# Weight preparation spread 4, 5 and 4 a tick, with the first weight loads held back, in a fused scan and two-MLP kernel

## The chip, the cores and the metric

The kernel runs on one core of a Trainium2 chip. A core has a matrix engine (TensorE, PE in the profile; the loading of its stationary operand is shown as PEld), a vector engine (VectorE, DVE), a scalar engine (ScalarE, ACT), a general engine (GpSimd, POOL) and a synchronisation engine (SyncE, SP). Each engine works through its own queue of instructions in order. DMA transfers are issued from the queues of SP, ACT and POOL. The metric is the device time of one execution in microseconds (us).

## The reference

Three computations follow one another. First a scan over a sequence of 768 positions for 4 batches and 8 heads, with a decay per position, in chunks:

```python
cum = np.cumsum(la, axis=-1)                       # la = log(clip(a))
L = np.exp(cum[:, :, :, None] - cum[:, :, None, :]) * causal
M = np.einsum('bhin,bhjn->bhij', Cc, Bc) * L
y_intra = np.einsum('bhij,bhjd->bhid', M, xc)
y_inter = np.einsum('bhin,bhnd->bhid', Cc, state) * decay_to_i[..., None]
...
state = decay_full[:, :, None, None] * state + np.sum(Bx, axis=2)
```

Its output, 3072 tokens of 256 numbers, goes through two layers in float32:

```python
h = x @ w_in                                       # 256 -> 2048
x = (np.maximum(h, 0.0) + alpha * np.minimum(h, 0.0)) @ w_out
gate = 1.0 / (1.0 + np.exp(-(x @ w_gate)))         # 256 -> 1536
out = (gate * (x @ w_val)) @ w_out2
```

## The kernel before, in words

The scan is cut into chunks of 96 positions (`T`), 8 per batch and 32 in all (`NCH`). The loop over `i` in 33 ticks works on them in a staggered way: in tick `i` VectorE makes the weighted scores `mt(i)` (`ev_weigh`, L324) and the state's factor `bd(i)` (L331), TensorE makes the decay `d(i+1)` (L298), which ScalarE turns into `lt(i+1)` by an exponential (L303), TensorE makes the output `yd(i-1)` (L346, L352), which ScalarE copies out as the next state (L359) and as the layer's input `x1` (L360), and TensorE makes the scores `cb(i+1)` (L317). The logarithms' running sum, called cum here, is made at the start for all chunks in two parts (`parts`). Its first three chunks go by small DMAs straight to `dl` and `dr` (`load_cum`, L261 and L262), the later ones through DRAM (`cum_d`). A small constant `pick` that the two parts need comes by a DMA from the tile `picks` (L548).

From tick `lead` = 7 on (`go` is true then; `at` counts the steps), the same ticks also hold steps of the first layer, one step per tick: `step_in` makes `h` for 512 tokens and 128 hidden columns (six matmuls, L391), then ScalarE and VectorE make `t` (L396), `g` (L398) and its two halves `gh` and `gl` (L407, L408), and `step_out` adds the step before into `acc` (six matmuls, L430). The first 16 steps use columns 0 to 1023 for token blocks 0 and 1 (`half` is 8 steps), the next 16 steps the other columns. After the 33 ticks the rest of the first layer and the second layer run without the scan.

The weights come in 64-bit floats and are made into two float32r parts on the chip. They are handled in groups (one 128x2x256 tile each, 512 KB of DMA): `queue` holds `win0, wout0, win1, wout1, ...`, 16 groups for the first layer (`first2`) and 18 for the second. `take_up` issues a group's load on the POOL queue (L118) into the ring `raw` of `RAWS` = 3 buffers. `work()` hands out one instruction, or nothing, of the conversion at a time, `OPS` = 7 to a group: handout 0 scales on ScalarE (`mag<-raw`, L130, the present group and the next one), 1 shifts (L155, or two at L158), 2 copies the high part on ScalarE (L145), 3 clips (L163), 4 makes the low part (L147), 5 and 6 put sign and bits together (L165, L170); 2 and 4 finish the group before. `feed(n, ...)` hands out n of them; `need(g)` hands out at once whatever group g still lacks. A `raw` buffer is free again after its handout 6, and `take_up` may be `RAWS` groups ahead.

What sets the order around the change is this written-out loop, nothing else: before tick 7 each tick hands out `EARLY` = 6 (3 after `ev_decay`, 3 at the tick's end), from tick 7 on 1 and 2.

Of the kernel before, what the change touches and what calls it, by code (L numbers as in the profile page):

```python
# [8 lines left out]
F32 = mybir.dt.float32  # L9
# [9 lines left out]
T = 96  # L19
# [8 lines left out]

WG = 256

RAWS = 3

OPS = 7

EARLY = 6

NX = 6
NC = 4
# [6 lines left out]
def kernel(  # L45
# [21 lines left out]
    nc = tc.nc  # L67
    NB, H, S = a.shape
    NT, DM = out.shape
# [13 lines left out]
    NR = NB * H  # L83


    KD = T + 2 + 2 * H

    bf = lambda t: t.bitcast(F32)
# [11 lines left out]
    x1 = cpool.tile([128, KT, NT], F32, name="x1")  # L100
# [12 lines left out]

    def take_up(most=RAWS):

        while taken[0] < min(len(queue), worked[0] // OPS + most):
            raw = ring.tile([128, 2, WG, 2], U32, tag="raw", name="raw", bufs=RAWS)
            nc.gpsimd.dma_start(  # L118
                out=raw.rearrange("p k f w -> p k (f w)"), in_=words(queue[taken[0]][1])
            )  # L120
            raws[taken[0]] = raw
            taken[0] += 1
# [11 lines left out]
    def work():  # L134


        g, op = divmod(worked[0], OPS)
        if g < len(queue):
            flips = queue[g][2]
            low, high = (raws[g][:, :, :, w] for w in range(2))  # L140
        if op in (2, 4):
            if g > 0:
                dst, m = queue[g - 1][0], mags[g - 1]
                if op == 2:
                    nc.scalar.copy(dst[:, 0], m)  # L145
                else:
                    nc.vector.tensor_tensor(dst[:, 1], m, bf(dst[:, 0]), op=ALU.subtract)  # L147
        elif g == len(queue):
            pass
        elif op == 0:  # L150
            scale(g)
            scale(g + 1)
        elif op == 1:
            if flips is None:
                nc.vector.tensor_scalar(low, low, 29, None, op0=ALU.logical_shift_right)  # L155
            else:
                for i in range(2):
                    nc.vector.tensor_scalar(  # L158
                        low[:, i], low[:, i], 29, flips[:, i:i + 1],
                        op0=ALU.logical_shift_right, op1=ALU.bitwise_xor,  # L160
                    )
        elif op == 3:
            nc.vector.tensor_scalar(mags[g], mags[g], TOP, -TOP, op0=ALU.min, op1=ALU.max)  # L163
        elif op == 5:
            nc.vector.scalar_tensor_tensor(  # L165
                low, high, 0x80000000, low, op0=ALU.bitwise_and, op1=ALU.bitwise_xor
            )
        else:
            m = mags[g].bitcast(U32)
            nc.vector.scalar_tensor_tensor(  # L170
                m, m, 3, low, op0=ALU.logical_shift_left, op1=ALU.bitwise_or
            )
        worked[0] += 1
        take_up()
# [4 lines left out]
    def feed(n, groups):  # L179

        for _ in range(n):
            if worked[0] < ready(groups - 1):
                work()
# [8 lines left out]
    first2 = len(queue)  # L192
# [7 lines left out]
    apool = actx.enter_context(tc.tile_pool(name="apool", bufs=1))  # L200
# [10 lines left out]
    left_c = misc[0:KD, T:T + W]  # L211
    eye_d = k_misc[0:N, c0 + T:c0 + T + N]
    pick = apool.tile([2 * NR, 1], F32, name="pick")
    picks = apool.tile([1, NR, 2], F32, name="picks")
    ones_t = apool.tile([2 * NR, T], F32, name="ones_t")

    parts = apool.tile([2 * NR, S], F32R, name="parts")

    a_t, cum = (x1[0:2 * NR, i, NT - S:NT] for i in range(2))
    xs = [apool.tile([W, H * (D + N)], F32, name=f"xs{i}") for i in range(NX)]  # L220
    dl = [apool.tile([KD, W], F32R, name=f"dl{i}") for i in range(NC)]
    dr = [apool.tile([KD, H, T], F32R, name=f"dr{i}") for i in range(NC)]
# [7 lines left out]
    def load_x(c):  # L230

        b, k = divmod(c, CPB)
        t = xs[c % NX]
        nc.sync.dma_start(out=t[0:T], in_=xb[b, k * T:(k + 1) * T, :])
        if k == 0:
            nc.gpsimd.memset(t[T:W, 0:H * D], 0.0)

    def load_bc(c):


        if c < ND:
            BC[c] = aring.tile([128, W + 4 * T], F32, tag="bc0", name="bct", bufs=3)
            nc.sync.dma_start(out=BC[c], in_=bc0[:, c])
        elif (c - ND) % G == 0:
            g = (c - ND) // G
            nc.sync.dma_start(
                out=bt[g % NG][:, :, 0:T], in_=bc[g][:, 0].rearrange("p (g t) -> p g t", t=T)
            )
            src = bc[g][:, 1].rearrange("(m q) t -> q m t", q=NP)
            dst = ct[g % NG].rearrange("(m q) b t -> q m b t", q=NP)  # L250
            for q in range(NP):
                nc.sync.dma_start(out=dst[q][:, q], in_=src[q])
# [34 lines left out]
    def store_cum():  # L287
        nc.sync.dma_start(
            out=cum_d.rearrange("b h l s -> (b h l) s"), in_=bf(parts)
        )  # L290
# [3 lines left out]
    def ev_decay(c):  # L294

        d = psum.tile([W, 2, 512], F32, tag="d", name="d")
        for e in range(2):
            nc.tensor.matmul(  # L298
                d[:, e, 0:4 * T], dl[c % NC], dr[c % NC][:, 4 * e:4 * e + 4, :],
                start=True, stop=True,  # L300
            )
        LT[c] = t = aring.tile([W, H, T], F32, tag="lt", name="lt", bufs=2)
        nc.scalar.activation(  # L303
            t.rearrange("j (e h) t -> j e (h t)", e=2), d[:, :, 0:4 * T], AF.Exp
        )
# [97 lines left out]
    def halves(key):  # L403
        g = gt[key]
        gh = ring.tile([128, BL], F32R, tag="gh", name="gh", bufs=3)
        gl = ring.tile([128, BL], F32R, tag="gl", name="gl", bufs=3)
        nc.scalar.copy(gh, g)  # L407
        nc.vector.tensor_tensor(gl, g, bf(gh), op=ALU.subtract)  # L408
        gt[key] = gh, gl
# [3 lines left out]
    half = NF1 // 2  # L413
# [53 lines left out]
    def moe2_out(k, f):  # L467
# [8 lines left out]
        if last:  # L476

            prods.sort(key=lambda v: v[1] // 2)
            sb = ring.tile([128, 2, 2, DM], F32, tag="raw", name="osb", bufs=RAWS)
        for n, (i, tt) in enumerate(prods):  # L480
# [24 lines left out]
    with tc.manual_schedule():  # L505
# [28 lines left out]
        def load_a(e, s):  # L534
            for l in range(2):
                e.dma_start(
                    out=a_t[l:2 * NR:2, s], in_=a.rearrange("b h s -> (b h) s")[:, s]
                )

        def load_eye(i):  # L540
            nc.gpsimd.dma_start(
                out=xs[i][T:W, H * D:].rearrange("s (h n) -> s h n", n=N),
                in_=eye_d.unsqueeze(1).broadcast_to([N, H, N]),
            )

        load_a(nc.sync, pieces[0])
        load_a(nc.scalar, slice(T, S))
        nc.gpsimd.dma_start(out=pick, in_=picks)  # L548
        nc.scalar.activation(warm[:, 0:1], ones_t[:, 0:1], AF.Ln)
        nc.sync.dma_start(out=misc, in_=k_misc[:, c0:])  # L550
        load_bc(0)
        load_x(0)
        load_eye(0)
        nc.gpsimd.dma_start(out=alpha_sb, in_=alpha)
        load_eye(1)
        take_up(1)
        nc.gpsimd.dma_start(out=units_c, in_=k_misc[:, 0:N])

        def setup_dl(i):
            nc.scalar.copy(dl[i], left_c)  # L560
# [36 lines left out]
        load_bc(1)  # L597
        load_cum(1)
        load_x(1)
        ev_decay(0)  # L600
        take_up(2)
        setup_dl(2)
# [6 lines left out]
        load_x(2)  # L609
        store_cum()  # L610
        load_eye(2)
        take_up()
        setup_dl(3)
        setup_mask(3, nc.scalar)
# [10 lines left out]
        at = 0  # L625
        for i in range(NCH + 1):
            go = i >= lead
            if i < NCH:
                ev_weigh(i)
            if i == 0:  # L630
                for j in range(NG):
                    nc.scalar.activation(
                        bt[j][:, :, T:W], units_c.unsqueeze(1).broadcast_to([128, G, N]),
                        AF.Copy, scale=2.0,
                    )
            if i + 3 < NCH:
                load_x(i + 3)
                load_bc(i + 3)
            if i + 4 < NCH:
                load_cum(i + 4)  # L640
            if at > 0:
                halves(steps[at - 1])
            if i + 1 < NCH:
                ev_decay(i + 1)
            feed(1 if go else EARLY // 2, first2)
            if go:
                step_in(at, "h")
            if i > 0:
                ev_out(i - 1)
            if i + 1 < NCH:  # L650
                ev_scores(i + 1)
            if go:
                if at > 0:
                    step_out(at - 1, two=False)
                splits(at)
                at += 1
            feed(2 if go else EARLY // 2, first2)

            if i == lead // 2:
                split_x("m1", 0, 0, BL // 2)  # L660
            if i == lead - 1:
                split_x("m1", 0, BL // 2, BL)

            if i == -(-2 * BL // T):
                split_x("m1", 1)
# [101 lines left out]
```

## Time and profile before

| | us |
|---|---|
| median of 3 runs | 669.73 |
| lowest and highest | 668.87 and 670.18 |
| profiled execution | 671.24 |
| its span | 669.5 |

| engine | busy us | share of the span |
|---|---|---|
| PE | 636.6 | 95% |
| DVE | 389.7 | 58% |
| ACT | 333.5 | 50% |
| POOL | 33.7 | 5% |

The profile shows one execution. The engines' busy times overlap, so they don't add up to the span; what an engine's idle time costs depends on the place where it lies. The granted clock is the share of TensorE's full speed: 1.00 is 2.4 GHz and 0.50 is 1.2 GHz.

### The profile page before, as it was taken

How to read it: one execution, taken by the hardware profiler on the slowest of the kernel's cores; microseconds unless marked ns; L12 is line 12 of the kernel's file. 1: busy time of each engine (PE TensorE's matmuls, PEld its weight loads, DVE VectorE, ACT ScalarE, POOL GpSimd, SP SyncE). 2: the span in 40 equal slices, each digit the busy share in tenths (PEclk: the TensorE clock that was granted, in tenths of full speed). 3: DMA queues.
4: the chain of work that ended last, by engine and by line, in shares of the span. 5: the costliest groups of instructions: out<-in, count | busy, mean ns of one | idle time of the engine just before them, and what ended most of it. 6: DMA issues, size and time to landing. Idle time of an engine off the chain costs nothing.

```text
span 669.5 us, 9604 instructions
## 1 busy us (share of the span) xinstructions
PE 636.6 (95%) x3744; PEld 503.6 (75%) x3744; DVE 389.7 (58%) x636; ACT 333.5 (50%) x628; POOL 33.7 (5%) x53
## 2 busy tenths in 40 slices
PE   1779999998999999999999999999999999999997
PEld 0336667675788888888888888888888888888885
DVE  5677768687688887888677433443433433433433
ACT  4667777766556666656556333332332333332322
POOL 6110100000000000000000000000000000000000
PEclk9769999999999999999999999999999999999999
DMA  5653333412112221121000000000000000000000
GB/s 171 205 149 111 89 114 93 124 54 64 31 34 63 64 63 37 58 64 64 0 1 0 1 1 0 32 0 1 33 0 1 32 0 1 32 0 1 32 1 31
DMA packets 19751, 31.03 MB, mean 46 GB/s; under 512 B 7418, under 2 KB 15226, under 8 KB 19706
## 3 DMA queue, kind: packets, MB, share of 16 engines
q0 software_dynamic: 5184, 17.89, 8.7%
q1 hardware_dynamic: 14394, 12.36, 6.4%
q8 instruction: 29, 0.48, 0.3%
q10 hardware_dynamic: 128, 0.18, 0.1%
q14 instruction: 16, 0.13, 0.1%
HBM read 27.04 MB, written 3.34 MB: 45 GB/s over the span
## 4 chain that ended last, share of the span: by engine, by line
PE 89%; DVE 3%; issue 2%; ACT 2%; DMA 2%; POOL 0%; ACTq 0%; SPq 0%; POOLq 0%; DVEq 0%
PE acc L430 20%; PE h L391 19%; PE gate L457 15%; PE val L457 15%; PE po L485 10%; PE po L490 5%; PE cb L317 3%; PE yd L352 1%; PE d L298 1%; DMA raw<-in_moe_w_out_dram 1%; PE yd L346 1%; DMA raw<-in_moe_w_in_dram 1%; DVE mt L324 1%; ACT xs L359 0%; DMA pick<-picks 0%
## 5 line engine op out<-in xcount | busy, mean ns | idle before, releaser
L391 PE MATMUL h<-xh,win 128*128 128x512 f32 x576 | 148.2, 393 | 3.1 <-ACT xh L382 1.7
L464 DVE TENSOR_TENSOR p<-val,s 128x512 f32<-128x512 f32 x72 | 49.8, 692 | 138.5 <-PE val L457 136.7
L391 PEld LDWEIGHTS h<-xh,win 128*128 128x128 f32 x576 | 109.0, 190 | 25.1 <-ACT xh L382 2.1
L430 PE MATMUL acc<-gh,wout 128*128 128x512 f32 x384 | 106.7, 400 | 1.8 <-DVE wout L147 1.8
L398 DVE SCALAR_TENSOR_TENSOR g<-h,salpha,t 128x512 f32<-128x512 f32 x96 | 72.0, 750 | 51.2 <-ACT t L396 50.8
L457 PE MATMUL gate<-xh,w2gate 128*128 128x512 f32 x360 | 92.8, 393 | 0.0
L430 PEld LDWEIGHTS acc<-gh,wout 128*128 128x128 f32 x384 | 70.6, 189 | 28.4 <-ACT t L396 10.0
L457 PE MATMUL val<-xh,w2val 128*128 128x512 f32 x360 | 91.4, 389 | 0.0
L407 ACT CAST gh<-p 128x512 fp32r<-128x512 f32 x72 | 44.6, 620 | 93.7 <-DVE p L464 93.7
L396 ACT ACTIVATE t<-h,sign 128x512 f32<-128x512 f32 x96 | 66.0, 688 | 50.5 <-PE h L391 50.0
L462 ACT ACTIVATE s<-gate 128x512 f32<-128x512 f32 x72 | 43.0, 597 | 92.8 <-PE gate L457 92.8
L407 ACT CAST gh<-g 128x512 fp32r<-128x512 f32 x96 | 59.6, 621 | 44.8 <-DVE g L398 44.8
L457 PEld LDWEIGHTS val<-xh,w2val 128*128 128x128 f32 x360 | 67.6, 188 | 14.3
L408 DVE TENSOR_TENSOR gl<-g,gh 128x512 fp32r<-128x512 f32 x96 | 66.1, 689 | 15.0 <-ACT gh L407 13.9
L408 DVE TENSOR_TENSOR gl<-p,gh 128x512 fp32r<-128x512 f32 x72 | 49.8, 691 | 41.2 <-ACT gh L407 41.1
L457 PEld LDWEIGHTS gate<-xh,w2gate 128*128 128x128 f32 x360 | 64.0, 189 | 10.6
L485 PE MATMUL po<-w2out,gh 128*128 128x512 f32 x240 | 64.2, 389 | 0.0
L430 PE MATMUL acc<-gl,wout 128*128 128x512 f32 x192 | 59.8, 393 | 0.0
L485 PEld LDWEIGHTS po<-w2out,gh 128*128 128x128 f32 x240 | 45.1, 188 | 9.3
L430 PEld LDWEIGHTS acc<-gl,wout 128*128 128x128 f32 x192 | 36.3, 189 | 7.8
L490 PEld LDWEIGHTS po<-w2out,gl 128*128 128x128 f32 x240 | 36.7, 189 | 4.7
L490 PE MATMUL po<-w2out,gl 128*128 128x256 f32 x240 | 38.1, 282 | 0.0
(83 smaller groups left out, 570.0 us busy)
## 6 DMA issues: line engine op xcount, KB each, us to landing
raw<-in_moe_w_out_dram POOLq DMA_DIRECT2D x14, 512.0 KB, 4.4
xs<-in_xb_dram SPq DMA_DIRECT2D x32, 144.0 KB
raw<-in_moe_w_in_dram POOLq DMA_DIRECT2D x8, 512.0 KB, 4.4
raw<-in_moe_w_gate_dram POOLq DMA_DIRECT2D x6, 512.0 KB, 4.1
raw<-in_moe_w_val_dram POOLq DMA_DIRECT2D x6, 512.0 KB, 4.1
out_dram<-osb SPq DMA_DIRECT2D x12, 256.0 KB
bt<-in_bc_dram SPq DMA_DIRECT2D x7, 192.0 KB
ct<-in_bc_dram SPq DMA_DIRECT2D x28, 48.0 KB
```

The costliest lines, as they stand in the source:

```text
L317: nc.tensor.matmul(cb[:, e, 0:4 * T], left, right, start=True, stop=True)
L391: nc.tensor.matmul(h, w[:, wl, kt, :], xh["m1", k][:, xl, kt, :], start=(i == 0 and kt == 0), stop=(i == 2 and kt == KT - 1),)
L396: nc.scalar.activation(t, h, AF.Identity, scale=sign[:, f:f + 1])
L398: nc.vector.scalar_tensor_tensor(g, h, salpha[:, f:f + 1], t, op0=ALU.mult, op1=ALU.max)
L407: nc.scalar.copy(gh, g)
L408: nc.vector.tensor_tensor(gl, g, bf(gh), op=ALU.subtract)
L430: nc.tensor.matmul(acc[k][:, m], w[:, wl, m * 128:(m + 1) * 128], g, start=(first and i == 0), stop=(last and i == 2),)
L457: nc.tensor.matmul(p, w[:, wl, kt, :], xh["m2", k][:, xl, kt, :], start=(i == 0 and kt == 0), stop=(i == 2 and kt == KT - 1),)
L462: nc.scalar.activation(s, gate, AF.Sigmoid)
L464: nc.vector.tensor_tensor(p, val, s, op=ALU.mult)
L485: nc.tensor.matmul(o[e][:, u].rearrange("p (l d) -> p l d", l=2), ph[:, ts], w, start=(f == 0), stop=False, skip_group_check=True,)
L490: nc.tensor.matmul(o[e][:, u, 0:DM], pl[:, ts], w[:, 0, :], start=False, stop=last, skip_group_check=True,)
```

## The change

There are four buffers for weights instead of three. Ticks before `lead` hand out 4 weight instructions (2 and 2) instead of 6, the first eight ticks with a step 5 (2 and 3) and the later ones 4 (2 and 2) instead of 3 (1 and 2). `picks` moves into an unused stretch of `x1`, and its DMA to the ScalarE queue. The first weight load is issued ahead of the small constants on POOL; the second and third stand behind two new copies on POOL that read the cum rows of chunk 1 and of chunk 2 (`seen`), so that they are issued when those rows have landed.

```diff
-RAWS = 3
+RAWS = 4
...
-EARLY = 6
+EARLY = 4
+FIRST = 5
+LATER = 4
...
-    picks = apool.tile([1, NR, 2], F32, name="picks")
...
+    picks = x1[0:1, 0, NT - S - 2 * NR:NT - S].rearrange("p (r l) -> p r l", l=2)
...
-        nc.gpsimd.dma_start(out=pick, in_=picks)
+        nc.scalar.dma_start(out=pick, in_=picks)
...
         load_x(0)
+        take_up(1)
         load_eye(0)
         nc.gpsimd.dma_start(out=alpha_sb, in_=alpha)
         load_eye(1)
-        take_up(1)
         nc.gpsimd.dma_start(out=units_c, in_=k_misc[:, 0:N])
+        seen = apool.tile([128, 2], F32, name="seen")
...
         load_bc(1)
         load_cum(1)
         load_x(1)
+
+        nc.gpsimd.tensor_copy(seen[T:KD, 0:1], bf(dl[1][T:KD, 0:1]))
         ev_decay(0)
         take_up(2)
...
         load_eye(2)
+        nc.gpsimd.tensor_copy(seen[T:KD, 1:2], bf(dl[2][T:KD, 0:1]))
         take_up()
...
-            feed(1 if go else EARLY // 2, first2)
+            now = EARLY if not go else FIRST if at < half else LATER
+            feed(now // 2, first2)
...
-            feed(2 if go else EARLY // 2, first2)
+            feed(now - now // 2, first2)
```

On POOL, from the constant `pick` or the zeroed state rows to the third weight load, before (`raw<-` is a weight load, the four `xs` DMAs and `units` are small constants):

```order
L548 DMA pick<-picks 64x1x1
L236 MEMSET xs_103 16x256
L541 DMA xs_103<-in_k_misc_dram 16x8x16
L554 DMA alpha_sb<-in_alpha_dram 128x16
L541 DMA xs_104<-in_k_misc_dram 16x8x16
L118 DMA raw<-in_moe_w_in_dram 128x2x512
L557 DMA units<-in_k_misc_dram 128x16
L118 DMA raw<-in_moe_w_out_dram 128x2x512
L541 DMA xs_105<-in_k_misc_dram 16x8x16
L118 DMA raw<-in_moe_w_in_dram 128x2x512
```

and now, where `dl_109` and `dl_110` are the tiles that hold the cum rows of chunks 1 and 2:

```order
L239 MEMSET xs_102 16x256
L121 DMA raw<-in_moe_w_in_dram 128x2x512
L544 DMA xs_102<-in_k_misc_dram 16x8x16
L558 DMA alpha_sb<-in_alpha_dram 128x16
L544 DMA xs_103<-in_k_misc_dram 16x8x16
L560 DMA units<-in_k_misc_dram 128x16
L605 COPY seen<-dl_109 18x1
L121 DMA raw<-in_moe_w_out_dram 128x2x512
L544 DMA xs_104<-in_k_misc_dram 16x8x16
L618 COPY seen<-dl_110 18x1
L121 DMA raw<-in_moe_w_in_dram 128x2x512
L121 DMA raw<-in_moe_w_out_dram 128x2x512
```

The first weight load has moved up, the next three stand behind a wait for a cum, and a fourth load follows the third at once.

On ACT, from `lt(2)` to `lt(4)` in the ticks without steps, before (`mag<-raw` is the instruction that waits for a weight load):

```order
L303 ACTIVATE lt<-d 112x768
L130 ACTIVATE mag<-raw 128x512
L359 COPY xs_104<-yd 16x2x32 x4
L360 COPY x_73<-yd 128x2x96
L145 CAST win_74<-mag 128x512
L303 ACTIVATE lt<-d 112x768
L130 ACTIVATE mag<-raw 128x512
L359 COPY xs_105<-yd 16x2x32 x4
L360 COPY x_73<-yd 128x2x96
L145 CAST wout_82<-mag 128x512
L303 ACTIVATE lt<-d 112x768
```

and now:

```order
L306 ACTIVATE lt<-d 112x768
L362 COPY xs_103<-yd 16x2x32 x4
L363 COPY x_73<-yd 128x2x96
L133 ACTIVATE mag<-raw 128x512
L306 ACTIVATE lt<-d 112x768
L148 CAST win_74<-mag 128x512
L362 COPY xs_104<-yd 16x2x32 x4
L363 COPY x_73<-yd 128x2x96
L306 ACTIVATE lt<-d 112x768
L362 COPY xs_105<-yd 16x2x32 x4
L363 COPY x_73<-yd 128x2x96
```

The `mag` of the fourth group, which stood between `lt(3)` and the copies of the state, is a tick later now; the `mag` of the third follows the copies.

On DVE, around the last group of `w_in` that the ticks use (`win_81`), before:

```order
L158 TENSOR_SCALAR raw<-raw,flip 128x256 x2
L324 TENSOR_TENSOR mt<-cb,lt 112x2x4x96
L331 TENSOR_TENSOR bd<-xs_108,lt 112x128
L408 TENSOR_TENSOR gl<-g,gh 128x512
L163 TENSOR_SCALAR mag<-mag 128x512
L147 TENSOR_TENSOR win_81<-mag,win_81 128x512
L398 SCALAR_TENSOR_TENSOR g<-h,salpha,t 128x512
```

and now:

```order
L161 TENSOR_SCALAR raw<-raw,flip 128x256 x2
L327 TENSOR_TENSOR mt<-cb,lt 112x2x4x96
L334 TENSOR_TENSOR bd<-xs_103,lt 112x128
L411 TENSOR_TENSOR gl<-g,gh 128x512
L166 TENSOR_SCALAR mag<-mag 128x512
L150 TENSOR_TENSOR win_81<-mag,win_81 128x512
L401 SCALAR_TENSOR_TENSOR g<-h,salpha,t 128x512
```

The rows are alike but stand at another place: `bd<-xs_108` belongs to chunk 29 and `bd<-xs_103` of the changed kernel (its `xs` are numbered one lower) to chunk 25, so `win_81` is made four ticks earlier.

## Rows read from the trace of the kernel before

**Rows 1.** The page, part 2: TensorE's granted clock in tenths, 40 slices.

```profile
PEclk9769999999999999999999999999999999999999
```

**Rows 2.** Waits of PE, 48 to 172 us: total us, times, longest us.

```profile
PE cb L317 <- DVE mt L324: 2.5, 3, 1.4
PE acc L430 <- DVE wout L147: 1.8, 1, 1.8
PE h L391 <- DVE win L147: 1.3, 1, 1.3
```

**Rows 3.** Timeline of ACT: start us, us, what, [idle before <-releaser].

```profile
20.51 0.81 ACT L303 ACTIVATE lt<-d 112x768 f32<-112x768 f32 x1 [0.58 <-ACT mag L130]
...
27.94 0.66 ACT L130 ACTIVATE mag<-raw 128x512 f32<-128x512 f32 x1 [3.63 <-DMA raw<-in_moe_w_out_dram]
...
43.17 0.67 ACT L130 ACTIVATE mag<-raw 128x512 f32<-128x512 f32 x1 [2.37 <-DMA raw<-in_moe_w_in_dram]
```

**Rows 4.** Timeline of DVE, the ticks without steps.

```profile
6.21 0.31 DVE L283 SCALAR_TENSOR_TENSOR parts<-x,pick 64x96 fp32r<-64x96 f32 x1 [1.10 <-DMA pick<-picks]
...
24.24 0.95 DVE L324 TENSOR_TENSOR mt<-cb,lt 112x768 f32<-112x768 f32 x1
...
25.30 0.69 DVE L165 SCALAR_TENSOR_TENSOR raw<-raw 128x512 uint32<-128x512 uint32 x1
...
27.30 0.95 DVE L324 TENSOR_TENSOR mt<-cb,lt 112x768 f32<-112x768 f32 x1
...
34.47 0.95 DVE L324 TENSOR_TENSOR mt<-cb,lt 112x768 f32<-112x768 f32 x1
...
41.58 0.95 DVE L324 TENSOR_TENSOR mt<-cb,lt 112x768 f32<-112x768 f32 x1
```

**Rows 5.** Timeline of PE: decay of chunk 1, the first step.

```profile
17.01 0.95 PE L298 MATMUL d<-dr,dl 114*112 114x384 f32 x2 [4.36 <-DMA dl<-parts]
...
46.95 2.93 PE L391 MATMUL h<-xh,win 128*128 128x512 f32 x6 [1.75 <-ACT xh L382]
```

**Rows 6.** Timeline of SP: the loads of chunk 1's and chunk 2's cum.

```profile
11.53 0.65 SPq L262 DMA_DIRECT2D dl<-parts  x1
...
14.38 0.56 SPq L262 DMA_DIRECT2D dl<-parts  x1
```

**Rows 7.** Tile raw, weight loads issued at 5 to 13 us: issue to landing.

```profile
DMA to landing us min/median/max: 4.2/6.8/7.3
```

**Rows 8.** Tile raw, weight loads issued at 20 to 30 us.

```profile
DMA to landing us min/median/max: 4.4/4.8/5.2
```

**Rows 9.** Windows: us, busy us (and count) of PE, PEld, DVE, ACT, POOL; PEclk, DMA, GB/s.

```profile
30.00:34.00 4.00, 4.00 (x69) 2.15 (x64) 2.67 (x6) 3.93 (x11) 0.71 (x1) 0.50 0.80 245
...
46.00:48.00 2.00, 1.05 (x3) 0.86 (x4) 1.97 (x4) 1.97 (x4) 0.35 (x1) 0.54 0.09 31
...
54.00:60.00 6.00, 6.00 (x71) 3.95 (x71) 4.79 (x9) 3.04 (x6) 0.00 (x0) 1.00 0.19 50
```

**Rows 10.** Chain of waits, after the wait for wout: start us, us, what.

```profile
165.67 2.93 PE acc L430 x6
168.60 1.63 PE h L391 x6
...
170.81 1.58 PE acc L430 x6
172.39 1.38 PE h L391 x6
```

**Rows 11.** Waits of DVE, 48 to 172 us.

```profile
DVE g L398 <- ACT t L396: 27.7, 22, 4.0
```

**Rows 12.** Timeline of DVE, then of PE: mt and the cb behind it.

```profile
61.27 0.95 DVE L324 TENSOR_TENSOR mt<-cb,lt 112x768 f32<-112x768 f32 x1
...
64.49 0.90 PE L317 MATMUL cb<-ct,bt 64*112 64x384 f32 x4
```

## The prediction

> **What bounds the kernel now.** I read the page first, then PE's waits, then the timelines of the first 60 us engine by engine, then windows.
>
> The page's clock line shows that TensorE runs at 0.9 to 1.0 from the fourth slice of 17 us on; only slices two and three, 17 to 50 us, are at 0.7 and 0.6 [rows 1]. The windows say the same from the other side: at 54 to 60 us, when steps of the first layer run beside the scan, PE is busy all 6.00 us at full clock, and little else can matter there [rows 9]. After 48 us the table of waits has three causes: `cb` waiting for `mt` (2.5 us in three places), `acc` for the weights `wout` (1.8 us, once) and `h` for the weights `win` (1.3 us, once) [rows 2]. So what this change can move lies before the first `h`, which starts at 46.95 us [rows 5], and in these 5.6 us.
>
> In the ticks without steps ACT is the engine to look at. It executes in order, and twice it stood still on a `mag` whose weight load had not landed: 3.63 us before 27.94 and 2.37 us before 43.17 [rows 3]. VectorE's `mt` marks the ticks: 24.24, 27.30, 34.47 and, two ticks on, 41.58 [rows 4]. The 7.17 us from the third to the fourth chunk hold the first stall; the next two ticks take 3.55 us each. The first `h` then comes 5.37 us after the last of these, with the second stall in between. In those ticks TensorE has the lower clock (0.50, busy 4.00 of 4 us at 30 to 34) [rows 9], so 3.55 us is a pace of TensorE at 1.2 GHz.
>
> **The change part by part.** All times are against the profiled execution: 671.24 us, of which 669.5 are its span. The median of the runs is 669.73, 1.5 lower; I take the same saving from both.
>
> *Pick and the start.* VectorE waited 1.10 us for `pick` before its instruction at 6.21 [rows 4]. On ACT that DMA is issued sooner, but it stands ahead of the table load and the logarithm there and delays them by about one issue (SP's take 0.56 and 0.65 [rows 6]). Half of the wait is what I count: cum is some 0.5 us earlier, which the next step uses.
>
> *The held loads.* Chunk 1's cum was issued at 11.53 [rows 6] and its `d` could start at 17.01 [rows 5]: 5.5 us for 6 KB. Three weight loads were in flight then, and themselves took 4.2 to 7.3 us [rows 7], against 4.4 to 5.2 later on [rows 8]. With two of them gone I put the landing 3 us after an issue at 11.0, so `d(1)` at 14. What that wins is mostly given back at once: the second weight load is now issued behind it, at about 14.3, lands 4.8 us later at 19.1, and ACT needs it for the second `mag` (0.6 us) ahead of `lt(2)`: 19.7 instead of 20.51 [rows 3]. The third load waits for chunk 2's cum, which SP issues 2.85 us after chunk 1's [rows 6]: issue near 17.2, landing at 22.0, and `lt(3)`, which stands behind its `mag`, at 22.7. A copy on POOL itself is next to nothing; queued behind it there are only weight loads and constants for chunks 2 to 5.
>
> *Four handouts instead of six, with four buffers.* The `mag` of the fourth group leaves its place between `lt(3)` and the copies of the state, stands a tick later, and its load is issued together with the third. From there on a load has two groups, 14 handouts or 3.5 ticks, where it had one group of 7 handouts, 1.2 ticks. Both stalls of [rows 3] go. VectorE gets lighter too: from 25.30 to 27.30 [rows 4] four weight instructions take 2.00 us, 0.50 each; five of seven handouts are VectorE's, so a handout costs it 0.36 us, and a tick loses 0.71. What is late next is TensorE at its lower clock. I place `mt(2)` at 21 (24.24), `mt(3)` at 25 (27.30), and then the 3.55 us pace: 28.6 (34.47), 32.1, 35.7 (41.58). From there to the first `h` 5.37 less 2.37, 3.0 us: 38.7. Against 46.95 that is 8.2 us.
>
> Its bounds: if cum takes 5.5 us as before and held loads take 7.3, the second lands at 24.1 and the third at 27.0, `lt(3)` starts at 27.6, `mt(3)` at 30, the first `h` at 43.7: 3.2 us. If TensorE reaches full clock in those ticks, VectorE is next, with four handouts (1.43) and `mt` and `bd` (24.24 to 25.30, 1.06): 2.5 us a tick, some 3.2 more over three ticks: 11.4 us.
>
> *The clock at the first step.* `h` came after 1.75 us of idle PE and took 2.93 us [rows 5], against 1.38 at full clock [rows 10]. With ACT's stall gone the idle time is shorter. Between 0 and 1.55 us; I take 0.8.
>
> *Five and four handouts with the steps.* Before, handouts ran out of time at the end: in the ticks of chunks 29 and 30, `need` had one and four instructions made in front of the matmuls, and PE waited 1.3 and 1.8 us [rows 2]. Now the last group is made four ticks earlier, so both waits go, 3.1 us. After the second one PE was at its lower clock again: `acc` 2.93 us where the next took 1.58, and `h` 1.63 against 1.38 [rows 10], which gives 1.6 more. Together 4.7 us; at least 3.1, if the clock falls at some other wait instead.
>
> *What VectorE has more of in those ticks.* Two more handouts in each of the first eight, 0.71 us, and one, 0.36, in the twelve after. VectorE waited for `t` 22 times, 27.7 us, 1.26 a tick on the mean [rows 11], and `mt`, ending at 62.22, had until 64.49, when the next `cb` took its turn: 2.27 us [rows 12]. So most ticks hide it. The three that don't are those in which `cb` waits already (2.5 us): there the handouts behind the step are another kind now, shorter in one, longer in the two others. I take 0.7 us of loss; the bounds are 1.0 of gain and 3.5 of loss (each of the three with a handout pair more, 0.7, and a fallen clock, 1.6, once).
>
> Sum: 8.2 + 0.8 + 4.7 - 0.7 = 13.0 us. 671.24 becomes 658.2, and the median of 669.73 becomes 656.7.
>
> **The rivals.**
>
> *The held loads land late.* The loads that ACT needs first are now issued in the middle of VectorE's work, at 14 to 18 us, and each behind a landing. For it: the early loads took up to 7.3 us [rows 7]; against it: loads issued into a busy VectorE at 20 to 30 us took 4.4 to 5.2 [rows 8]. By the lower bound above, and half the clock term: 3.2 + 0.4 + 4.7 - 0.7 = 7.6 us, 662.1. The Trainium skill speaks for this one ("SBUF — State Buffer", "SBUF: two separate sides"): a DMA issued from the GpSimd queue has its descriptors written by GpSimd, which certain VectorE instructions lock out. By that rule the held loads would be the slow ones; [rows 8] doesn't bear it out, since those loads were not slower than the early ones.
>
> *The clock comes up early.* A TensorE without gaps from 21 us on may be at full clock in ticks 3 to 6. For it: 54 to 60 us without a gap are at 1.00; against it: 30 to 34 us, as full, are at 0.50 [rows 9]. 11.4 + 1.55 + 4.7 - 0.7 = 17.0 us: 652.8.
>
> *VectorE becomes the bound in the ticks with steps (slower).* One mechanism: the third handout behind the step pushes `mt` past the turn of `cb`, PE waits in each of the 20 ticks with more handouts, and TensorE's clock falls with the gaps, as it did at 46 to 48 us, where PE had 1.05 us of work in 2 and the clock was 0.54 [rows 9]. Price: 8 x 2 + 12 = 28 handouts of 0.36 on the path, 10.1 us, and six falls of 1.6, 9.6 us: 13.0 gained less 19.7 is 6.7 slower, 676.4. It decides where `mt` ends more than 2.27 us later than now. Two handouts give 0.71, so it takes something else as well.
>
> *The change doesn't do what it says.* Chunk 1's cum is late for another reason than the weight loads, the held loads then run exactly as late as ACT's stalls were long, and the waits at the end reappear at `mt`: no difference, 669.7. [Rows 7] against [rows 8] speak against it, and the removed handouts are gone from these ticks in any case.
>
> **How the numbers follow.** The forecast has 0.56, late loads 0.18, the early clock 0.12, VectorE as the bound 0.07, no effect 0.07. The likeliest case gives 656.7 us, with 654 to 660 around it. From 652.5 to 664.5 lie the forecast, most of the late loads with their own spread of 2 us, and half of the early clock: 0.8. What a measurement of this kernel can tell from no change is about 0.2%, 1.3 us. Faster by more: the first three and a little of the last, 0.88. Within it: 0.05. Slower: 0.07.
>
> **What would show it.** The first `h` at 37 to 41 us, and no `mag` on ACT idle for more than 1 us after 25 us; `d(1)` at 13.5 to 15 with a cum that lands in about 3 us; the second `mag` still waiting for its load near 19. At the end no wait of `h` for `win` or of `acc` for `wout`, and no low clock at 0.50 around the last chunks. `cb` waiting for `mt` for 2 to 4 us in all. I am wrong if the first `h` comes after 44 us, if `cb` waits for `mt` in more than six ticks, or if PE, after its 32nd step, is not as steady as before: then something outside the scan's ticks has moved.

## The result and the profile after

The changed kernel takes 658.8 us (median of 4 runs, 657.88 to 659.65) against 669.3 for the kernel before on the same chip: a ratio of 0.984, 95% interval 0.982 to 0.987. It is 10.5 us faster, where 13.0 were forecast: the forecast of 656.7 lies 2.1 us under the measured time, and the measured time lies inside the range of 652.5 to 664.5. The profiled execution took 659.65 us, its span 657.9, 11.6 less than before.

The page's clock line, part 2, now shows 0.9, 0.8 and 0.9 in the slices from 16 to 66 us, where [rows 1] had 0.7, 0.6 and 0.9:

```profile
PEclk9989999999999999999999999999999999999999
```

The table of PE's waits from 48 to 172 us, to be read beside [rows 2], has one row left. `h` and `acc` wait for no weights, and `cb` waits about as long as before in all (2.4 against 2.5 us), 0.3 us of it in a new place:

```profile
PE cb L320 <- DVE mt L327: 2.4, 4, 1.3
```

The start went another way than forecast. The timeline of PE (start us, us, what, [idle before <-releaser]) with the decays of chunks 1, 2 and 3, the scores `cb` of chunk 3 and the first two `h`, beside [rows 5]:

```profile
12.94 0.95 PE L301 MATMUL d<-dr,dl 114*112 114x384 f32 x2 [1.61 <-DMA dl<-parts]
...
17.88 0.95 PE L301 MATMUL d<-dr,dl 114*112 114x384 f32 x2 [0.74 <-DMA dl<-parts]
...
24.30 0.95 PE L301 MATMUL d<-dr,dl 114*112 114x384 f32 x2 [2.93 <-DMA dr<-cum_d]
...
27.39 1.62 PE L320 MATMUL cb<-bct 64*112 64x384 f32 x4 [1.15 <-DVE win L150]
...
42.77 1.67 PE L394 MATMUL h<-xh,win 128*128 128x512 f32 x6 [1.00 <-ACT xh L385]
...
46.22 1.55 PE L394 MATMUL h<-xh,win 128*128 128x512 f32 x6
```

Chunk 1's decay is 4.1 us earlier, and chunk 3's waits 2.93 us for a load that it didn't wait for before. DVE's `parts`, then its `mt(2)`, `mt(3)`, `mt(4)` and `mt(6)`, beside [rows 4]:

```profile
5.59 0.31 DVE L286 SCALAR_TENSOR_TENSOR parts<-x,pick 64x96 fp32r<-64x96 f32 x1
...
21.48 0.96 DVE L327 TENSOR_TENSOR mt<-cb,lt 112x768 f32<-112x768 f32 x1 [1.81 <-PE cb L320]
...
29.04 0.96 DVE L327 TENSOR_TENSOR mt<-cb,lt 112x768 f32<-112x768 f32 x1 [1.67 <-PE cb L320]
...
33.85 0.95 DVE L327 TENSOR_TENSOR mt<-cb,lt 112x768 f32<-112x768 f32 x1
...
39.32 0.96 DVE L327 TENSOR_TENSOR mt<-cb,lt 112x768 f32<-112x768 f32 x1 [0.58 <-PE cb L320]
```

`mt(2)` is 2.8 us earlier than before, `mt(3)` 1.7 us later, `mt(4)` 0.6 and `mt(6)` 2.3 us earlier. What stood in the way at `mt(3)` is seen on the queues. POOL issued the held loads so:

```profile
12.94 0.37 POOL L605 COPY seen<-dl 18x1 f32<-18x1 f32 x1 [5.96 <-DMA dl<-parts]
13.41 0.71 POOL L121 DMA_DIRECT2D raw<-in_moe_w_out_dram  x1
...
17.86 0.18 POOL L618 COPY seen<-dl 18x1 f32<-18x1 f32 x1 [3.19 <-DMA dl<-parts]
18.33 0.73 POOL L121 DMA_DIRECT2D raw<-in_moe_w_in_dram  x1 [0.28 <-issue]
19.06 0.72 POOL L121 DMA_DIRECT2D raw<-in_moe_w_out_dram  x1
```

and the chain of waits shows the load of chunk 3's cum (issued by SP at 19.71) right behind the second and third of them:

```profile
19.71 4.46 DMA dr<-cum_d
24.16 0.14 issue
24.30 0.96 PE d L301 x2
```

### The profile page after: what moved, and what is told of

It reads as the page before. It is cut to its first block, busy times and chain, and to the rows that moved or that the text cites. A ratio compares the mean times of both kernels' runs of the same rounds, so it can differ in the third digit from the quotient of the medians.

```text
span 657.9 us, 9595 instructions
## 1 busy us (share of the span) xinstructions
PE 631.5 (96%) x3744; PEld 500.2 (76%) x3744; DVE 389.2 (59%) x636; ACT 333.5 (51%) x628; POOL 33.5 (5%) x54
## 4 chain that ended last, share of the span: by engine, by line
PE 89%; DVE 5%; ACT 3%; issue 1%; DMA 1%; ACTq 0%
PE acc L433 20%; PE h L394 19%; PE gate L460 15%; PE val L460 15%; PE po L488 10%; PE po L493 5%; PE cb L320 3%; PE d L301 1%; DVE mt L327 1%; PE yd L355 1%; DMA dr<-cum_d 1%; PE yd L349 1%; ACT xs L362 1%; DVE raw L168 0%; DVE x L278 0%
```

## Experiments

Theory A: the handouts are the gain (fewer before the steps, an earlier end behind them), and the hold only moves a collision of weight loads with a small load of cum from chunk 1 to chunk 3. Its rivals: the hold earns the start (B), the later handouts come back as waits of `cb` (C), the fourth buffer does it (D). Each ratio is against the kernel before on the same chip: 669.14 us for the first four experiments, 669.13 for the next four, 669.54 for the last three.

**No hold (e1).**

```diff
-        nc.gpsimd.tensor_copy(seen[T:KD, 0:1], bf(dl[1][T:KD, 0:1]))
...
-        nc.gpsimd.tensor_copy(seen[T:KD, 1:2], bf(dl[2][T:KD, 0:1]))
```

> The changed kernel without its two copies on POOL: the second to fourth weight loads are issued as soon as POOL comes to them, everything else as changed. Theory A (the hold only moves a collision of weight loads with a cum load, from chunk 1's to chunk 3's): within 1.5 us of the changed kernel's 658.8; the decay of chunk 1 starts near 17 us instead of 12.94, the wait of the decay of chunk 3 for its cum (2.9 us) is gone, the first h is within 1.5 us of 42.8. Theory B (the hold earns the gain before the first step): 662 to 664, first h near 46 to 47.

657.63 us, ratio 0.9826 (0.9806 to 0.9847). PE's timeline:

```profile
17.43 0.95 PE L301 MATMUL d<-dr,dl 114*112 114x384 f32 x2 [6.51 <-DMA dl<-parts]
...
23.04 0.60 PE L301 MATMUL d<-dr,dl 114*112 114x384 f32 x2
...
41.91 1.64 PE L394 MATMUL h<-xh,win 128*128 128x512 f32 x6 [1.07 <-ACT xh L385]
```

Chunk 1's decay is 4.5 us later than with the hold, chunk 3's 1.3 us earlier and without a wait of its own, the first `h` 0.9 us earlier. The time is within theory A's 1.5 us and not clear of the changed kernel's. B falls.

**Later handouts alone (e2)**, on the kernel before:

```diff
+FIRST = 3
+LATER = 4
...
+            now = EARLY if not go else FIRST if at < half else LATER
```

> The kernel before with only the handouts of the later ticks changed: 6 a tick before the steps and 3 in the first eight ticks with a step as before, 4 after them instead of 3. Theory A (the two waits for weights at the end and the low clock behind them are 4.8 us of the gain by themselves): 669.3 less 4.8 is 664.5, first h still at 47, no wait of h for win or of acc for wout. Rival C (VectorE gives the handouts back as waits of cb for mt): 668 to 670, those waits up by 3 us or more.

665.59 us, ratio 0.9942 (0.9922 to 0.9961): a gain of 2.6 to 5.2 us, 3.9 in the middle; the 4.8 that was expected lies inside the interval. The first `h` starts at 47.35. Of PE's waits after the first `h`, `cb` for `mt` is left in three places (0.38, 1.51, 0.51 us, 2.4 together, as before), so C falls. The waits of ACT up to 48 us show both stalls still there:

```profile
ACT mag L132 <- DMA raw<-in_moe_w_out_dram: 3.3, 2, 2.3
ACT mag L132 <- DMA raw<-in_moe_w_in_dram: 3.3, 2, 2.6
```

**Handouts alone (e3)**, on the kernel before:

```diff
-EARLY = 6
+EARLY = 4
+FIRST = 5
+LATER = 4
```

> The kernel before with 4, 5 and 4 handouts, but three buffers, no hold, and pick on POOL as before. Theory A (fewer handouts before the steps give a load 1.75 ticks, which is enough): ACT's stalls on a weight load after 25 us are under 1 us in all, the first h at 42 to 44, 659 to 661. Theory D (the fourth buffer does it): stalls of 3 us or more stay, first h at 45 to 47, 663 to 665.

656.74 us, ratio 0.9814 (0.9794 to 0.9833), below the 659 to 661 of theory A. ACT waits 0.9 us for a weight load, once. PE's timeline:

```profile
17.03 0.95 PE L300 MATMUL d<-dr,dl 114*112 114x384 f32 x2 [4.70 <-DMA dl<-parts]
...
39.49 1.65 PE L393 MATMUL h<-xh,win 128*128 128x512 f32 x6 [1.07 <-ACT xh L384]
```

`h` starts 7.5 us earlier than before, also below the 42 to 44 us expected, with chunk 1's cum as late as ever. D falls: three buffers do. The early handouts without the late ones were not run; by the medians, this kernel less e2 puts them at about 8.9 us.

**Three buffers (e4)** in the changed kernel:

```diff
-RAWS = 4
+RAWS = 3
```

> The changed kernel with three buffers instead of four; hold, pick and handouts as changed. Theory A: 658 to 660.5, the same within 1.5 us. Theory D (the fourth buffer does it): 662 or more, with ACT waiting 2 us or more for weight loads after 25 us. A third outcome: faster than the changed kernel, since the fourth load no longer runs beside chunk 3's cum; then its decay starts before 24 us.

657.86 us, ratio 0.9831 (0.981 to 0.9851): the same. Chunk 3's decay starts at 23.17 us, 1.1 earlier, and the first `h` at 40.38: the third outcome in the trace but not clear in the time.

**The first copy alone (e5).**

```diff
-        nc.gpsimd.tensor_copy(seen[T:KD, 1:2], bf(dl[2][T:KD, 0:1]))
```

> The changed kernel with the first of its two copies on POOL alone: the third and fourth weight loads follow the second at once, at 14 to 16 us. Theory A (a hold moves the collision on to the next small load): the decay of chunk 3 no longer waits 2.9 us for dr, but the cum of chunk 2 and the store of cum to DRAM, issued at 13.9 and 15.6, run beside three weight loads; 657 to 659. Theory B2 (the second copy alone does harm, the first helps): 655 to 656.5, first h at 40 or earlier.

658.97 us, ratio 0.9849 (0.9831 to 0.9866), as theory A has it in time, but not in place: it expected chunk 3's wait to go and chunk 2's cum to be late. The collision is at chunk 3's cum again, and longer, through the store: SP issues the load behind it at 22.75 us, where it was 19.28.

```profile
25.47 0.95 PE L301 MATMUL d<-dr,dl 114*112 114x384 f32 x2 [4.52 <-DMA dl<-cum_d]
```

**Old handouts, all else changed (e6).**

```diff
-EARLY = 4
-FIRST = 5
-LATER = 4
+EARLY = 6
+FIRST = 3
+LATER = 3
```

> The changed kernel with 6, 3 and 3 handouts as before; hold, four buffers and pick as changed. Theory A (the handouts are the gain): 667 to 670, no different from before, with the waits of h for win and of acc for wout back at the end. Theory D (buffers and hold are worth something when loads are needed faster): 663 to 666, with the first h at 43 to 45 and only the waits at the end back.

666.02 us, ratio 0.9948 (0.9932 to 0.9964). Theory A was too strict here, and D has it almost to the number: with six handouts a tick, the rest of the change (hold, fourth buffer, `pick`, the earlier first load) is worth 2.4 to 4.6 us. The first `h` starts at 44.31, and ACT waits 4.7 us for weight loads, all before 23 us, at the two loads that are held. The waits at the end are back as they were:

```profile
PE acc L433 <- DVE wout L150: 1.8, 1, 1.8
PE h L394 <- DVE win L150: 1.3, 1, 1.3
```

**Chunk 3's cum loaded directly (e7)**, in the changed kernel:

```diff
-    DIRECT = 3
+    DIRECT = 4
```

> The changed kernel with chunk 3's cum loaded directly from parts like the first three (DIRECT 4 instead of 3), so that it is issued near 16 us, ahead of the third and fourth weight loads, and not behind the store to DRAM. Theory A (the held loads collide with chunk 3's cum, 2.9 us on the path): its decay starts before 22.5 us instead of 24.30, first h 1.5 to 3 us earlier, 655.5 to 657.5. Rival E (bct and ct loads beside the held loads are late as well and take its place): 658 to 659.5, with cb waiting for a DMA.

657.47 us, ratio 0.9822 (0.9807 to 0.9838). PE's timeline:

```profile
20.94 0.98 PE L301 MATMUL d<-dr,dl 114*112 114x384 f32 x2
26.05 0.95 PE L301 MATMUL d<-dr,dl 114*112 114x384 f32 x2 [1.14 <-DMA dr<-cum_d]
...
29.30 1.62 PE L320 MATMUL cb<-ct,bt 64*112 64x384 f32 x4 [1.31 <-DMA dr<-cum_d]
...
40.71 1.66 PE L394 MATMUL h<-xh,win 128*128 128x512 f32 x6 [1.07 <-ACT xh L385]
```

The decay of chunk 3 is 3.4 us earlier, chunk 4's now waits 1.14 us for its cum, `h` is 2.1 us earlier. The trace has the collision on the path, and part of it moves on once more; the time alone is not clear of the changed kernel's. Rival E's sign is there too: chunk 4's `cb` waits 1.31 us for a DMA. But it also does so without a hold (1.80 us with the handouts alone).

**Handouts, pick on ACT, chunk 3 direct (e8)**, on the kernel before:

```diff
+EARLY = 4
+FIRST = 5
+LATER = 4
...
-    DIRECT = 3
+    DIRECT = 4
...
+        nc.scalar.dma_start(out=pick, in_=picks)
```

> The kernel before with 4, 5 and 4 handouts, three buffers, no hold, pick on ACT and DIRECT 4. If the two small changes add to the handouts: 654.5 to 656, below the 656.7 of the handouts alone; the decay of chunk 1 still waits to about 16.5 us. If cum of chunk 1 under three weight loads is the only limit of the start: 656 to 657.5, the same.

655.82 us, ratio 0.980 (0.9783 to 0.9817), the lowest of all, and its interval lies just below that of the changed kernel (0.982 to 0.987). Against the handouts alone it is not clear of noise.

**Hold, three buffers, chunk 3 direct (e9)**: the changed kernel with `RAWS = 3` and `DIRECT = 4`.

> The changed kernel with three buffers and with chunk 3's cum loaded directly (the two edits of e4_three_buffers and e7_cum3_direct together), the hold kept. Theory A (the hold wins 4 us at chunk 1 and loses them at the loads that it collides with): with the collisions cleared it beats the handouts without a hold, 653.5 to 655, first h before 38.5. Theory F (the hold cannot win, since ACT needs the second and third loads at their old places): 655.5 to 657.5, ACT waits 3 us or more for weight loads before 30 us.

656.15 us, ratio 0.9803 (0.9785 to 0.982). F's number, and its wait: ACT stands still for weight loads for 5.7 us in four places, 3.8 us of it before 30 us. With the collision at chunk 3's cum cleared, no difference shows between the kernel with the hold and the one without (e8).

**Three later handouts (e10)** in the fastest kernel:

```diff
-LATER = 4
+LATER = 3
```

> e8_handouts_direct with 3 handouts instead of 4 in the ticks after the first eight steps, so that three instructions of the last wout are again made in front of a matmul. Theory A (waits at the end and the clock behind them are the late part of the gain): 1 to 3.5 us above e8's 655.8, with one wait of acc for wout of 1 to 1.8 us, first h as there. Rival C (the later handouts are free either way): the same within 0.7.

658.82 us, ratio 0.9841 (0.9823 to 0.9859): 0.4% or 2.7 us above it, and the first outcome. One wait for weights is back, with the lower clock behind it (four matmuls of `acc` take 1.19 us at the full clock):

```profile
154.54 2.07 PE L432 MATMUL acc<-gh,wout 128*128 128x512 f32 x4 [1.88 <-DVE wout L149]
```

The start of this kernel is instruction for instruction that of the one before, and yet on another chip its first `h` came at 40.33 instead of 38.69. From 28 to 35 us TensorE's granted clock was 1.00 in that kernel and 0.51 in this one, by the windows (as in [rows 9]):

```profile
28.00:35.00 7.00, 5.07 (x82) 2.36 (x82) 6.17 (x13) 5.99 (x16) 1.16 (x3) 1.00 0.69 188
28.00:35.00 7.00, 6.42 (x68) 3.03 (x72) 4.68 (x9) 3.25 (x9) 0.89 (x2) 0.51 0.71 195
```

So one profile tells starts apart to some 1.6 us, no better, and the smaller differences of a first `h` above are not shown by it alone.

**3, 6 and 4 handouts (e11)** in the fastest kernel:

```diff
-EARLY = 4
-FIRST = 5
+EARLY = 3
+FIRST = 6
```

> e8_handouts_direct with 3, 6 and 4 handouts: one fewer in each tick before the steps, one more in each of the first eight with one. If VectorE and ACT still hold the early ticks up: first h 0.5 to 1.5 us earlier, 654.5 to 655.8. If the sixth handout of 0.36 us uses up the slack of mt in the ticks with steps: cb waits for mt in more than five ticks there, 656.5 to 659.

658.72 us, ratio 0.9836 (0.9818 to 0.9853): slower, as the second expectation has it, though not by the wait named: `cb` waits for `mt` in four places, not in more than five. The first `h` stays at 38.65. With a sixth handout a tick and three buffers, a weight load (issued at 46.17) is needed sooner than it lands; ACT stands still for it, `t` and `g` come late behind it, and PE waits before the fourth step. ACT's line, then PE's:

```profile
51.60 0.66 ACT L132 ACTIVATE mag<-raw 128x512 f32<-128x512 f32 x1 [3.61 <-DMA raw<-in_moe_w_in_dram]
...
53.67 1.66 PE L393 MATMUL h<-xh,win 128*128 128x512 f32 x6 [1.84 <-DVE g L400]
```

In the table the last column is the difference of the medians; where the text has a range, it is that of the ratio.

| kernel | handouts | buffers | hold | us | us against before |
|---|---|---|---|---|---|
| before | 6, 3, 3 | 3 | no | 669.1 to 669.5 | |
| changed | 4, 5, 4 | 4 | both | 658.8 | -10.5 |
| e1 | 4, 5, 4 | 4 | no | 657.6 | -11.5 |
| e2 | 6, 3, 4 | 3 | no | 665.6 | -3.6 |
| e3 | 4, 5, 4 | 3 | no | 656.7 | -12.4 |
| e4 | 4, 5, 4 | 3 | both | 657.9 | -11.3 |
| e5 | 4, 5, 4 | 4 | first | 659.0 | -10.2 |
| e6 | 6, 3, 3 | 4 | both | 666.0 | -3.1 |
| e7, direct | 4, 5, 4 | 4 | both | 657.5 | -11.7 |
| e8, direct | 4, 5, 4 | 3 | no | 655.8 | -13.3 |
| e9, direct | 4, 5, 4 | 3 | both | 656.2 | -13.4 |
| e10, direct | 4, 5, 3 | 3 | no | 658.8 | -10.7 |
| e11, direct | 3, 6, 4 | 3 | no | 658.7 | -10.8 |

## Why the prediction was right, and where it was not

*Pick.* VectorE's instruction went from 6.21 to 5.59, 0.6 us, where 0.5 was counted.

*The held loads: the step that failed.* `d(1)` came at 12.94, still better than the 14 of the forecast, and the second load landed in time for a `mag` at 17.54. Of the three weight loads that the prediction has in flight at 11.53 in the kernel before, two were: the first, issued at 6.33, had landed 4.2 us later. But the prediction said that behind the copies on POOL there are only weight loads and constants, and looked at who waits on POOL. It did not ask which transfers the held loads run beside once they are let go: chunk 3's cum, which goes through DRAM and is issued at 19.71, took 4.46 us beside them. So `lt(3)` started at 25.34, not 22.7. A second load was late beside them and kept `mt(3)` until 29.04, not 25: `lt(3)` had ended at 26.15, but chunk 3's `cb` started only at 27.39. The page puts its wait of 1.15 us down to `win`, which `cb` doesn't read. What it does read is the 248 KB of `bct`, issued at 20.43, whose last part landed at 27.25 by the trace; with three buffers the page itself names that load:

```profile
25.75 1.62 PE L320 MATMUL cb<-bct 64*112 64x384 f32 x4 [0.64 <-DMA bct<-in_bc_dram]
```

The experiments without a hold and with chunk 3 direct show the collision from both sides. The rival of the late loads had the place and the direction (its 662.1 is too high); in place of weight loads that land late, it was the loads beside them that they delay.

*Four handouts.* Both of ACT's stalls of [rows 3] went, as argued, and three buffers are enough for it; two shorter ones are those that the hold makes:

```profile
17.54 0.67 ACT L133 ACTIVATE mag<-raw 128x512 f32<-128x512 f32 x1 [2.00 <-DMA raw<-in_moe_w_out_dram]
...
22.57 0.66 ACT L133 ACTIVATE mag<-raw 128x512 f32<-128x512 f32 x1 [1.52 <-DMA raw<-in_moe_w_in_dram]
```

The fourth buffer was counted as part of that gain; the runs show none for it beside four handouts. The pace after `mt(4)` was not 3.55 us but 2.74 (33.85 to 39.32 in two ticks), with TensorE at the full clock in part of them: the window of 30 to 34 us, which [rows 9] has at 0.50, is at 1.00, and the two behind it are at 0.66 and 0.91.

```profile
30.00:34.00 4.00, 3.33 (x70) 1.71 (x62) 2.59 (x7) 3.79 (x10) 1.02 (x2) 1.00 0.47 123
34.00:38.00 4.00, 3.14 (x40) 1.49 (x40) 4.00 (x8) 2.49 (x8) 0.00 (x0) 0.66 0.80 257
38.00:42.00 4.00, 3.77 (x47) 1.65 (x44) 3.42 (x8) 3.86 (x13) 0.71 (x1) 0.91 0.66 190
```

So a part of what was lost at `mt(3)` came back, as the rival of the early clock had it. From 25 to 45 us the granted clock was 0.57 before, 0.66 in e2 with its six handouts, 0.91 in the changed kernel, and 0.83 to 1.00 in all the others. How much of the earlier start is the clock and how much the stalls, no run separates. The first `h` starts at 42.77: 4.2 us instead of 8.2, inside the bounds of 3.2 and 11.4.

*The clock at the first step: mis-sized.* 0.8 us was taken, with 1.55 as the upper bound, from the first `h` alone. Before, `h`, `yd`, `cb` and `d` up to the second `h` all ran at the lower clock; from first to second `h` it was 53.06 less 46.95, 6.1 us, and is 46.22 less 42.77, 3.5 now. That is 2.7 us, above the bound. The second `h` before:

```profile
53.06 1.55 PE L391 MATMUL h<-xh,win 128*128 128x512 f32 x6
```

*The late part.* Where the steps run on without the scan, `h` started at 175.67 before and starts at 164.18 now, 11.5 us earlier (the first line is from before); at the second `h` it was 6.8. So 4.7 us came in between, where 4.7 less 0.7 was forecast: both waits gone (3.1), the low clock behind them gone (1.6), and the waits for `mt` at 2.4 instead of 2.5. The loss of 0.7 didn't come, because one of the three waits got shorter by more than another got longer (1.38 to 0.48, and 0.70 to 1.34). The experiment with these handouts alone has 3.9 us, and taking one away costs 2.7.

```profile
175.67 2.91 PE L391 MATMUL h<-xh,win 128*128 128x512 f32 x12
...
164.18 2.91 PE L394 MATMUL h<-xh,win 128*128 128x512 f32 x12
```

4.2, 2.7 and 4.7 make 11.6 us, the difference of the two spans. That the sum of 13.0 came so near is in part luck: 4.0 us too much at the start stand against 1.9 too little for the clock and 0.7 too little at the end. The other 1.1 us are the medians, which differ by 10.5. Of the signs named, the first `h` missed its 37 to 41 us and stayed under 44; ACT's waits after 25 us and the waits for weights at the end went as said. The slower rival didn't show: the fifth handout left `mt` in time. The sixth doesn't test it, since what it cost came through a weight load.

## What to carry to other kernels

Holding a large load back until a small one has landed moves it beside the next small one: before adding such a wait, list what is issued in the 5 us after it is let go. Where an engine in order stops for a load, giving it less of that work per tick can do more than another buffer. And a preparation that is finished by force just in front of its use cost the wait here (3.1 us in two places), and then the clock behind it (1.6 us).

## What the runs showed of the hardware

A small transfer was held up by the large ones beside it. Before, `d(1)` started at 17.01, 5.5 us after the issue of the 6 KB of chunk 1's cum at 11.53, with two 512 KB loads in flight (issued at 7.65 and 8.90, landed 6.8 and 7.3 us later). In the changed kernel it started at 12.94, 1.9 us after the issue at 11.03, when the only weight load before it had landed (issued at 3.75, 5.2 us). Without the hold the issue was at 10.88 and `d(1)` at 17.43. And two executions of the same start, on two chips, differ by 1.6 us at the first `h`, and in TensorE's granted clock from 28 to 35 us (1.00 and 0.51).
